# Quarter products in all groups, weights' sums moved into the first layer

## The chip, the cores and the metric

One core of one Trainium2 chip. The metric is the device time of one execution in microseconds (us).

## The reference

Attention in chunks of 32 positions with some context and 8 memory positions, over 4 x 768 tokens and 8 heads of 64; then two layers on its 3072 x 512 result:

```
x = attention(q, k, v, mem_k, mem_v)      # 3072 x 512
h = maximum(x @ w_in, 0)
x = (h * h) @ w_out                       # 512 -> 2048 -> 512
h = x @ w_in2
g = maximum(h, 0) + log1p(exp(-abs(h)))
out = g @ w_out2                          # 512 -> 2048 -> 512
```

All is float32. The kernel splits each operand into a high and a low part that TensorE multiplies fast (F32R) and makes three products for each (low x high, high x high, high x low).

## The kernel before

Tokens go in six blocks of 512 (NB); the second layer joins two blocks to a group (NGR = 3). TensorE (PE) works through block 0 and 1 of the first layer in steps f = 0..15, one tile of 128 hidden columns each, then blocks 2 to 5 in slots (n, p), p = 0..7, two tiles each, then the second layer, which has a first and a second product for each group.

Quarter products: a product of 2 x 2 quarters needs eight quarter products; with sums of quarters of activations and of weights made beforehand, seven do (`order` lists the seven, `quarter` in the first layer and `product` in the second make one). In the kernel before the slots, the first products of all groups and the second products of groups 1 and 2 (`second_stage`) go that way; group 0's second product (`plain_stage`, L1177) makes all eight. In `plain_stage` the sums of the output weights for the later groups are made as well (`add`, `weight_sums`) and stored to DRAM (`wsum`); its 16 weights' tiles come in 8 loads of 1 MB (`wo`), while `second_stage` uses 14 loads of 1 MB. Loads of weights go through four places in turn (`fetch`); x of the next group is loaded and split inside the second product (`next_x`).

The weights of the second layer arrive as 64-bit numbers and are turned into 32-bit ones by three operations (`rebias` on ScalarE, two in `r_join` on VectorE). For the input weights `in_jobs` (L594) does this during the slots of blocks 2 to 4, with the four sums (`four`) and four splits, each with a cast on ScalarE, a subtraction on VectorE and stores. For the output weights `out_jobs` (L648) does it during block 5's eight slots, without sums. `sum_jobs` (L574) makes the sums of the first layer's own weights during block 1's steps; in each slot `sum_load` fetches four of them (`wx`) into one fixed place each. The work buffers of all these are cf0, cf1 and cf2.

All DMAs are issued by SyncE (SP), in one order. VectorE (DVE), ScalarE (ACT) and SP each run their instructions in order too. From block 1's steps on, the instructions are recorded first (class `Recorder`) and then played in an order that is written out by hand as a list of numbers (MOVES, three parts: up to the middle of slot (4, 7), from there to the second layer, and the second layer's first two pairs). Recorded instructions carry L154, the line that plays them, in the profile; the line numbers of `g_split` and its like are those of helpers (`halves` L551, `low_half` L546).

Of the kernel before, what the change touches and what calls it, by code (L numbers as in the profile page):

```python
# [14 lines left out]
ALU = mybir.AluOpType  # L15
# [32 lines left out]
AHEAD = 1  # L48
SOFT_A = ((), (0,), (1, 2), (3, 4), (5, 6), (7, 8), (9, 10), (11, 12))
# [62 lines left out]
""",  # L112
    """
# [10 lines left out]
""",  # L124
    """
42 12 11 12 4 0 14 0 2 3 6 1 1 2 0 0 -38 -31 -24
# [4 lines left out]
class Recorder:  # L131
# [10 lines left out]
    def play(self, moves):  # L142
        jobs, self.jobs = self.jobs, None
        moves = iter(moves.split())
        at, order = 0, []
        for i, (engine, job) in enumerate(jobs):
            if engine is self.nc.tensor:
                order.append((at + 0.5, i))
                at += 1
            else:  # L150
                order.append((at + int(next(moves, 0)), i))
        for _, i in sorted(order):
            engine, job = jobs[i]
            ins = job().ins  # L154
            tile_ = (job.keywords["out"] if "out" in job.keywords else job.args[0]).tensor
            if hasattr(tile_, "tag"):
                name, by, first = self.last.get(tile_.tag, (None, None, None))
                if name != tile_.name:
                    if first is not None and by is not engine:
                        why = mybir.DependencyInfo(mybir.DependencyClass.Sync, mybir.DependencyReason.DATA)  # L160
                        self.tc.add_manual_dep(ins, first.name, why, reason="turn")
                    self.last[tile_.tag] = tile_.name, engine, ins
# [11 lines left out]
def body(ctx: ExitStack, tc: tile.TileContext, qk, vW, w1, w2, out):  # L174
# [347 lines left out]
    wsum = [dram.tile([P, KP, 2, QW], F32R, name=f"wsum{i}") for i in range(4)]  # L522
# [9 lines left out]

    def r_abs(f, top, low):
        rebias(f, top)
# [26 lines left out]
    def split(k, x, *stores):  # L561
        t = cf_tile(k, (P, 2, 2, QW), F32R)
        halves(t[:, :, 0], t[:, :, 1], x, *[(o, t[:, i]) for o, i in stores], late=True)
# [10 lines left out]
    def sum_jobs(p):  # L574
# [13 lines left out]
        def casts():  # L588
            split(kc, d["s"][:, 0:2], (wx[p][:, 0:2], slice(0, 2)))
            split(ka, d["s"][:, 2:4], (wx[p][:, 2:4], slice(0, 2)))  # L590
# [3 lines left out]
    def in_jobs(p):  # L594
        d = {}

        def load(i):
            d["r", i] = r_load(i, 2 * p + i, 0)

        def start(i):  # L600
            if i == 0:
# [769 lines left out]
```

## Time and profile before

| | us |
|---|---|
| median of 3 runs | 1068.08 |
| lowest, highest | 1067.32, 1069.87 |
| the profiled execution | 1067.74 |
| its span, first to last instruction | 1066.0 |

The profile is one execution. Its span is what the views below divide; 1.74 us of the execution's time lie outside it. PE is TensorE's products, PEld its weight loads, which overlap them. The granted clock is 0.998 over the span.

### The profile page before, as it was taken

The numbers are of one execution on the slowest core, as the hardware profiler recorded it, in microseconds if no ns is written. First come the engines' busy times: TensorE is split into PE (matmuls) and PEld (weight loads), VectorE is DVE, ScalarE is ACT, GpSimd is POOL, SyncE is SP. The second block draws the span as 40 slices with busy tenths as digits, with TensorE's granted clock in tenths as the row PEclk, the third lists the DMA queues.
The fourth block names the chain that finished last, engine by engine and source line by source line (L and its number), as shares of the span: only waits on it lengthen the run. The fifth ranks groups of instructions, "written<-read, shape, count | busy, mean of one in ns | idle before, by whom it ended". The sixth has DMA issues, their size and how long they took to land.

```text
span 1066.0 us, 20067 instructions
## 1 busy us (share of the span) xinstructions
PE 1046.4 (98%) x8072; PEld 886.2 (83%) x8072; DVE 767.0 (72%) x1321; ACT 589.7 (55%) x989; POOL 0.7 (0%) x6
## 2 busy tenths in 40 slices
PE   5999999999999999999999999999999999999998
PEld 5788888888888888888898788888788888888886
DVE  6877488788877778866584566967377886477953
ACT  3776554475576567547785654433355545354442
POOL 0000000000000000000000000000000000000000
PEclk9999999999999999999999999999999999999999
DMA  9764253478778678847999645865755757565762
GB/s 359 273 247 163 66 190 136 157 237 295 232 236 292 214 238 254 277 139 226 324 307 345 210 148 177 272 220 166 265 203 200 279 198 257 192 203 180 248 207 99
DMA packets 95196, 238.03 MB, mean 223 GB/s; under 512 B 8064, under 2 KB 40832, under 8 KB 87936
## 3 DMA queue, kind: packets, MB, share of 16 engines
q1 hardware_dynamic: 95104, 236.75, 65.6%
q8 instruction: 64, 1.05, 0.4%
q14 instruction: 28, 0.23, 0.1%
HBM read 184.29 MB, written 52.43 MB: 222 GB/s over the span
## 4 chain that ended last, share of the span: by engine, by line
PE 93%; DVE 3%; DMA 2%; issue 1%; ACT 1%; SPq 0%; ACTq 0%; DVEq 0%
PE acc L154 21%; PE bk L1173 19%; PE bk L1093 19%; PE hq L154 15%; PE hp L154 4%; PE acc L476 4%; PE xs L154 3%; PE bk L154 2%; PE hp L430 2%; PE hp L431 1%; PE hp L432 1%; DVE gl L546 1%; DMA wsum<-cf 1%; PE sc L271 1%; DVE h L1110 1%
## 5 line engine op out<-in xcount | busy, mean ns | idle before, releaser
L154 PE MATMUL acc<-g,w 128*128 128x512 f32 x984 | 257.4, 394 | 0.7 <-ACT g L154 0.3
L1173 PE MATMUL bk<-gh,ws 128*128 128x512 f32 x704 | 217.1, 390 | 0.1
L1093 PE MATMUL bk<-xo,ws 128*128 128x512 f32 x930 | 212.0, 389 | 1.0 <-DMA ws<-wb 1.0
L1093 PEld LDWEIGHTS bk<-xo,ws 128*128 128x128 f32 x930 | 174.5, 188 | 37.6 <-DVE h L1101 1.4
L154 PEld LDWEIGHTS acc<-g,w 128*128 128x128 f32 x984 | 173.9, 189 | 31.0 <-DVE g L154 1.6
L1173 PEld LDWEIGHTS bk<-gh,ws 128*128 128x128 f32 x704 | 131.9, 188 | 28.6 <-ACT cf L1280 0.9
L154 PEld LDWEIGHTS hq<-xe,w 128*128 128x128 f32 x1056 | 140.4, 190 | 11.4 <-ACT r L154 1.9
L154 PE MATMUL hq<-xe,w 128*128 128x256 f32 x1056 | 145.2, 283 | 0.5 <-ACT r L154 0.5
L1173 PE MATMUL bk<-gl,ws 128*128 128x512 f32 x352 | 137.1, 389 | 0.2 <-DVE gl L546 0.2
L546 DVE TENSOR_TENSOR gl<-h,gh 128x1024 fp32r<-128x1024 f32 x72 | 87.8, 1222 | 39.4 <-ACT gh L551 39.1
L551 ACT CAST gh<-h 128x1024 fp32r<-128x1024 f32 x72 | 75.9, 1054 | 68.3 <-PE bk L1173 67.3
L154 ACT ACTIVATE r<-r 128x512 f32<-128x512 f32 x144 | 91.1, 633 | 18.1 <-DVE r L154 15.8
L154 DVE TENSOR_TENSOR g<-r,g 128x512 fp32r<-128x512 f32 x80 | 54.9, 687 | 36.7 <-ACT g L154 36.2
L154 DVE STREAM_TRANSPOSE pt<-t 32x128 f32<-32x128 f32 x256 | 77.5, 303 | 4.2
L154 ACT COPY r<-hq 128x256 f32<-128x256 f32 x128 | 47.2, 369 | 56.8 <-PE hq L154 52.3
L1173 PEld LDWEIGHTS bk<-gl,ws 128*128 128x128 f32 x352 | 66.1, 188 | 14.5 <-DVE gl L546 0.8
L154 DVE TENSOR_TENSOR cf<-cf 128x256 f32<-128x256 f32 (+2 forms) x128 | 65.1, 537 | 8.4 <-ACT cf L154 7.7
L1100 ACT ACTIVATE cf<-cf 128x1024 f32<-128x1024 f32 x47 | 49.9, 1063 | 33.2 <-DVE cf L1099 33.2
L1099 DVE TENSOR_SCALAR cf<-h 128x1024 uint32<-128x1024 uint32 x47 | 32.6, 693 | 42.8 <-ACT h L1114 41.7
L1101 DVE SCALAR_TENSOR_TENSOR h<-h,cf 128x1024 f32<-128x1024 f32 x47 | 57.2, 1218 | 3.4 <-ACT cf L1100 3.4
L154 ACT CAST cf<-cf 128x512 fp32r<-128x512 f32 x64 | 37.5, 592 | 28.4 <-DVE cf L154 19.1
L154 DVE TENSOR_TENSOR r<-hq,r 128x256 f32<-128x256 f32 x96 | 40.3, 421 | 14.5 <-ACT r L154 8.8
(129 smaller groups left out, 1249.5 us busy)
## 6 DMA issues: line engine op xcount, KB each, us to landing
w<-wx SPq DMA_DIRECT2D x128, 256.0 KB, 4.4
ws<-wa SPq DMA_DIRECT2D x24, 1024.0 KB, 7.0
ws<-wo SPq DMA_DIRECT2D x20, 1024.0 KB, 5.9
ws<-wb SPq DMA_DIRECT2D x24, 768.0 KB, 4.3
r<-w SPq DMA_DIRECT2D x16, 1024.0 KB, 6.8
cf<-w SPq DMA_DIRECT2D x32, 512.0 KB, 6.3
ws<-wsum SPq DMA_DIRECT2D x16, 1024.0 KB, 5.2
qk<-qk SPq DMA_DIRECT2D x44, 336.0 KB, 5.3
```

The source lines that it names most:

```text
L154: ins = job().ins
L271: nc.tensor.matmul(out=sv[(2 * c + r) * 32:(2 * c + r + 1) * 32, j, w, i, :], lhsT=t[d, 2 * i + r, c * CHUNK:(c + 1) * CHUNK], rhs=t[d, 2 ...
L430: nc.tensor.matmul(out=hp, lhsT=b, rhs=xh[:, c], start=(c == 0), stop=False)
L431: nc.tensor.matmul(out=hp, lhsT=a, rhs=xl[:, c], start=False, stop=False)
L476: nc.tensor.matmul(out=acc[m][:, cols], lhsT=a, rhs=b, start=(f == 0 and j == 0 and cols.start == 0), stop=(f == KF - 1 and j == 2),)
L546: nc.vector.tensor_tensor(out=lo, in0=x, in1=hi.bitcast(F32), op=ALU.subtract)
L551: nc.scalar.copy(out=hi, in_=x)
L1093: nc.tensor.matmul(out=bk, lhsT=a, rhs=b, start=(start and n == 0), stop=(n == 5), skip_group_check=not start)
L1099: nc.vector.tensor_scalar(z.bitcast(U32), h.bitcast(U32), 1 << 31, None, op0=ALU.bitwise_or)
L1100: nc.scalar.activation(out=z, in_=z, func=AF.Softplus)
L1101: nc.vector.scalar_tensor_tensor(out=h, in0=h, scalar=0.0, in1=z, op0=ALU.max, op1=ALU.add)
L1173: nc.tensor.matmul(out=bk, lhsT=a, rhs=b, start=(start and j == 0), stop=(stop and j == 2), skip_group_check=more)
```

## The change

Group 0's second product uses `second_stage` like the others, and `plain_stage` is gone, with its sums of weights. All of the output weights' preparation is in the first layer now: `in_jobs` and `out_jobs` are replaced by `word_jobs`, sixteen rounds of one pair of tiles each (8 for the input weights, 8 for the output weights with their sums), recorded at the slots that WORDS lists. Rounds take turns between two sets of buffers, cf0 to cf2 and cf3 to cf5. POOL's scratch area for DMAs is cut to 1024. All three parts of MOVES are new, and `play` reads them differently: before, a number counted PE's instructions from the place of recording; now it counts places in the list of all recorded instructions, and PE's instructions fill what is left, in their order of recording. `wsum` is one tensor, and the second sum and the third have changed places in it.

```
+WORDS = [2 * r for r in range(11)] + [24, 25, 27, 28, 30]
...
 MOVES = (
...
+492 504 522 522 526 531 575 595 537 528 548 610 615 623 630 700 716 722 712 718 723 728 6 12 8 15 24 -16 -10 3 9 14 25
...
+28 35 41 39 45 21 22 -22 0 12 22 -1125 -1130 -1024 -1040 -922 -1032 -1049 -939 -902 -755 -751 -888 -904 -874 -859 -870
+-764 -761 -747 -731 -726 -725 -707 -697 -629 2 5 11 17 -65 -39 -24 -14 22 4 11 9 16 24 8 17 22 -101 -82 -69 -58 27 16
...
+26 38 36 18 28 -1250 -1257 -1159 -1154 -1147 -1176 -1160 -1155 -1137 -1119 -1117 -1125 -1150 -1146 -1142 -1094 -1017
+-1013 -1071 -1016 -1010 -945 -937 -878 -884 1 21 23 30 39 2 9 11 12 44 20 29 24 30 35 28 31 37 -19 -8 15 28 -21 -9 15
...
     def play(self, moves):
         jobs, self.jobs = self.jobs, None
         moves = iter(moves.split())
-        at, order = 0, []
-        for i, (engine, job) in enumerate(jobs):
-            if engine is self.nc.tensor:
-                order.append((at + 0.5, i))
-                at += 1
-            else:
-                order.append((at + int(next(moves, 0)), i))
-        for _, i in sorted(order):
+        order = [None] * len(jobs)
+        for i, (engine, _) in enumerate(jobs):
+            if engine is not self.nc.tensor:
+                order[i + int(next(moves, 0))] = i
+        rest = (i for i, (engine, _) in enumerate(jobs) if engine is self.nc.tensor)
+        for i in order:
+            i = next(rest) if i is None else i
...
+    def word_jobs(r):
+        layer_in, r = r < KP, r % KP
+        part = 0 if layer_in else 1
+        q, j = divmod(r, 2)
+        tiles = (2 * r, 2 * r + 1) if layer_in else (4 * q + j, 4 * q + 2 + j)
+        ka, kb, kc = ((0, 1, 2), (3, 4, 5))[r % 2]
+        f = None
+        raws = [r_load(k, t, part) for k, t in zip((ka, kb), tiles)]
+        f = cf_tile(kc)
+        for i in range(2):
+            rebias(f[:, i], raws[i][0])
+            r_join(f[:, i], *raws[i])
+        f = f.rearrange("p i (h q) -> p i h q", h=2)
+        s = cf_tile(ka, (P, 4, QW))
+        if layer_in:
             four(s, f)
...
+            split(kb, f[:, :, 1], (wb[r][:, 0:2], slice(0, 2)))
             t = f[:, 1].bitcast(F32R)
...
+            halves(t[:, 0], t[:, 1], f[:, 0, 0], (wa[r][:, 0], t))
+            split(kb, s[:, 0:2], (wa[r][:, 1:3], slice(0, 2)))
+            split(kc, s[:, 2:4], (wa[r][:, 3:4], slice(0, 1)), (wb[r][:, 2:3], slice(1, 2)))
+        else:
+            four(s, f.rearrange("p i h q -> p h i q"))
+            split(kb, f[:, :, 0], (wo[:, 0, 2 * q:2 * q + 2, j], slice(0, 2)))
+            t = f[:, 0].bitcast(F32R)
+            halves(t[:, 0], t[:, 1], f[:, 1, 1], (wo[:, 1, 2 * q + 1, j], t))
+            split(kb, s[:, 0:2], (wsum[:, 0:2, r], slice(0, 2)))
+            split(kc, s[:, 2:4], (wsum[:, 2:4, r], slice(0, 2)))
...
             old = life.pop() if life else None
-            jobs = (jobs2 if n < NB - 1 else jobs3) if here else []
+            if here:
+                at_slot = (n - 2) * KP + p
+                for r in [r for r in range(2 * KP) if WORDS[r] == at_slot]:
+                    word_jobs(r)
...
-        sums = {4: 0, 5: 1, 6: 2, 2: 3}
+        sums = {4: 0, 5: 1, 6: 3, 2: 2}
...
-                if grp > 0 and f % 4 == 3:
+                if f % 4 == 3:
...
-                (second_stage if grp else plain_stage)(grp, first_stage(grp))
+                second_stage(grp, first_stage(grp))
...
-    nc = bacc.Bacc("TRN2", target_bir_lowering=False, num_devices=1)
+    nc = bacc.Bacc("TRN2", target_bir_lowering=False, num_devices=1, dynamic_dma_scratch_size=1024)
```

A round records 25 instructions that are not PE's. The rows of numbers shown end with round 0's, and hold round 1's (-1125 to -629) and round 3's (-1250 to -884).

## Rows read from the trace of the kernel before

**Rows 1.** Page of the profile: busy us, share of the span, instructions of each engine.

```profile
PE 1046.4 (98%) x8072; PEld 886.2 (83%) x8072; DVE 767.0 (72%) x1321; ACT 589.7 (55%) x989; POOL 0.7 (0%) x6
```

**Rows 2.** Busy time by stage: length, then PE, PEld, DVE, ACT, POOL (instructions), clock, DMA.

```profile
0.00:124.00 124.00, 110.71 (x1440) 91.95 (x1441) 89.11 (x146) 77.94 (x130) 0.70 (x6) 0.99 0.64 233
124.00:220.00 96.00, 96.00 (x902) 78.98 (x901) 75.94 (x173) 47.69 (x87) 0.00 (x0) 1.00 0.47 162
220.00:316.00 96.00, 95.75 (x1119) 85.16 (x1117) 77.67 (x185) 61.02 (x124) 0.00 (x0) 1.00 0.76 249
...
508.00:604.00 96.00, 95.12 (x551) 82.59 (x550) 55.15 (x102) 66.85 (x128) 0.00 (x0) 1.00 0.90 301
...
831.00:909.00 78.00, 77.78 (x342) 63.65 (x341) 61.81 (x68) 40.75 (x50) 0.00 (x0) 1.00 0.72 255
```

**Rows 3.** The chain that ended last: start, length, engine and products.

```profile
609.12 57.12 PE bk L1093 x252
...
670.32 73.79 PE bk L1173 x324
```

**Rows 4.** PE in order of time: the slots' first product, and two slots of block 5.

```profile
218.96 0.87 PE L154 MATMUL hq<-xe,w 128*128 128x256 f32 x6
...
487.05 1.60 PE L154 MATMUL hq<-xe,w 128*128 128x256 f32 x12
...
497.61 1.59 PE L154 MATMUL hq<-xe,w 128*128 128x256 f32 x12
```

**Rows 5.** PE in order of time: first products of the three second stages.

```profile
666.07 0.62 PE L1173 MATMUL bk<-gh,ws 128*128 128x512 f32 x2
...
830.88 0.62 PE L1173 MATMUL bk<-gh,ws 128*128 128x512 f32 x2
...
984.05 0.62 PE L1173 MATMUL bk<-gh,ws 128*128 128x512 f32 x2
```

**Rows 6.** All engines in order of time, end of group 0; in brackets idle time and releaser.

```profile
755.32 0.32 SPq L525 DMA_DIRECT2D wsum<-wq  x1
...
761.14 0.60 SPq L525 DMA_DIRECT2D ws<-wb  x1
...
766.86 1.40 PE L1093 MATMUL bk<-xo,ws 128*128 128x512 f32 x5 [1.01 <-DMA ws<-wb]
```

**Rows 7.** DVE's and ACT's groups by form: count, busy us, mean ns of one.

```profile
L154 DVE TENSOR_TENSOR cf<-cf 128x512 fp32r<-128x512 f32 x56 | 38.0, 688 | 8.0 <-ACT cf L154 7.7
L154 DVE TENSOR_TENSOR cf<-cf 128x256 f32<-128x256 f32 x64 | 25.0, 419 | 0.4
L154 DVE SCALAR_TENSOR_TENSOR cf<-cf 128x512 uint32<-128x512 uint32 x32 | 21.8, 688 | 3.1 <-ACT cf L154 2.7
...
L154 DVE TENSOR_SCALAR cf<-cf 128x512 uint32<-128x512 uint32 x32 | 13.6, 424 | 10.1 <-DMA w<-wx 3.9 <-DMA cf<-w 3.6 <-DMA wo<-cf 2.5
...
L154 DVE TENSOR_TENSOR cf<-cf 128x256 fp32r<-128x256 f32 x8 | 3.3, 415 | 0.0
...
L154 ACT CAST cf<-cf 128x512 fp32r<-128x512 f32 x56 | 34.3, 620 | 28.1 <-DVE cf L154 18.7 <-DMA wb<-cf 4.1 <-DVE s L317 2.0
```

**Rows 8.** Busy time by stage, columns as in rows 2: the stretch in block 1.

```profile
157.00:196.00 39.00, 39.00 (x385) 32.11 (x383) 31.46 (x73) 18.67 (x33) 0.00 (x0) 1.00 0.37 129
196.00:212.00 16.00, 16.00 (x174) 13.12 (x159) 13.44 (x35) 6.52 (x14) 0.00 (x0) 1.00 0.49 161
```

**Rows 9.** The same in stretches of 12 us: two of DVE's fullest.

```profile
220.00:232.00 12.00, 11.75 (x134) 10.16 (x133) 11.61 (x28) 7.59 (x16) 0.00 (x0) 1.00 0.60 192
...
316.00:328.00 12.00, 12.00 (x79) 10.72 (x73) 11.63 (x31) 10.03 (x21) 0.00 (x0) 1.00 0.79 263
```

**Rows 10.** Waits of SP's queue: total us, times, longest.

```profile
SPq L154 <- DVE cf L154: 60.3, 38, 9.7
```

**Rows 11.** DMA issues: count, KB each, median us to landing.

```profile
w<-wx SPq DMA_DIRECT2D x128, 256.0 KB, 4.4
```

**Rows 12.** Instructions on wsum: duration ns (min, median, max), first and last start us.

```profile
L525 SPq DMA_DIRECT2D ws<-wsum x16: 320/332/887, 837.9 to 1043.2; - x16
```

More of the change, by code (lines that the diff above doesn't have):

```diff
@@ L75 @@
     """
[36 rows of a table removed]
-""",
-    """
[10 rows of a table removed]
[41 rows of a table added]
+""",
+    """
[12 rows of a table added]
 """,
     """
-42 12 11 12 4 0 14 0 2 3 6 1 1 2 0 0 -38 -31 -24
+6 1 2 2 2 2 -26 2 4 4 4 4 4 4 4 3 -52 -48 -43
 """,
@@ L521, in body @@
     wo = dram.tile([P, 2, KP, 2, 2, QW], F32R, name="wo")
-    wsum = [dram.tile([P, KP, 2, QW], F32R, name=f"wsum{i}") for i in range(4)]
+    wsum = dram.tile([P, 4, KP, 2, QW], F32R, name="wsum")
     def store(out, in_):
@@ L531, in r_load @@
         return v[:, :, 1], v[:, :, 0]
-    def r_abs(f, top, low):
-        rebias(f, top)
     def r_join(f, top, low):
@@ L559, in flush, with split @@
             lows.pop(0)()
-    def split(k, x, *stores):
+    def split(k, x, *stores, late=False):
         t = cf_tile(k, (P, 2, 2, QW), F32R)
-        halves(t[:, :, 0], t[:, :, 1], x, *[(o, t[:, i]) for o, i in stores], late=True)
+        halves(t[:, :, 0], t[:, :, 1], x, *[(o, t[:, i]) for o, i in stores], late=late)
     def four(s, f):
@@ L588, in casts @@
         def casts():
-            split(kc, d["s"][:, 0:2], (wx[p][:, 0:2], slice(0, 2)))
-            split(ka, d["s"][:, 2:4], (wx[p][:, 2:4], slice(0, 2)))
+            split(kc, d["s"][:, 0:2], (wx[p][:, 0:2], slice(0, 2)), late=True)
+            split(ka, d["s"][:, 2:4], (wx[p][:, 2:4], slice(0, 2)), late=True)
         return [((), (), (words,), ()), ((), (), (sums,), (casts,))]
[L594 to L601, printed above, removed]
-                d["f"] = cf_tile(2)
-            r_abs(d["f"][:, i], *d["r", i])
-        def join(i):
-            r_join(d["f"][:, i], *d["r", i])
-        def sums():
-            f = d["f"].rearrange("p i (h q) -> p i h q", h=2)
-            s = d["s"] = cf_tile(0, (P, 4, QW))
+    def word_jobs(r):
[13 more added lines that the diff above has]
+        if layer_in:
@@ L611, in sums @@
             four(s, f)
-        def casts():
-            f = d["f"].rearrange("p i (h q) -> p i h q", h=2)
-            split(1, f[:, :, 1], (wb[p][:, 0:2], slice(0, 2)))
+            split(kb, f[:, :, 1], (wb[r][:, 0:2], slice(0, 2)))
             t = f[:, 1].bitcast(F32R)
-            halves(t[:, 0], t[:, 1], f[:, 0, 0], (wa[p][:, 0], t), late=True)
-        def last():
-            split(1, d["s"][:, 0:2], (wa[p][:, 1:3], slice(0, 2)))
-            split(2, d["s"][:, 2:4], (wa[p][:, 3:4], slice(0, 1)), (wb[p][:, 2:3], slice(1, 2)))
@@ L623, in call @@
-        def call(fn, *a):
-            return (lambda: fn(*a),)
-        return [
-            (call(load, 0), (), (), ()),
-            (call(load, 1), call(start, 0), call(join, 0), ()),
-            ((), call(start, 1), call(join, 1), ()),
-            ((), (), (sums,), (casts,)),
-            ((), (), (), (last,)),
-        ]
-    out_raw = {}
-    def out_place(f, shape, dtype):
-        if f % 3 < 2:
-            return cf_tile(f % 3, shape, dtype)
-        return late[0].tile(list(shape), dtype, tag="cf", name="cf")
@@ L641, in out_load @@
-    def out_load(f):
-        if f < KF:
-            t = out_place(f, (P, DM), I64)
-            nc.sync.dma_start(out=t, in_=w2[f][:, DM:])
-            v = t.bitcast(U32).rearrange("p (n t) -> p n t", t=2)
-            out_raw[f] = v[:, :, 1], v[:, :, 0]
-    def out_jobs(f):
-        d = {}
-        def start():
-            d["x"] = cf_tile(2, (P, DM))
-            r_abs(d["x"], *out_raw[f])
-        def join():
-            r_join(d["x"], *out_raw.pop(f))
-        def cast():
-            t = out_place(f, (P, 2, 2, QW), F32R)
-            halves(t[:, :, 0], t[:, :, 1], d["x"].rearrange("p (m q) -> p m q", m=2), (wo[:, :, f // 2, f % 2], t), late=True)
-        return (lambda: out_load(f + 1),), (start,), (join,), (cast,)
+            halves(t[:, 0], t[:, 1], f[:, 0, 0], (wa[r][:, 0], t))
@@ L664, in body @@
     jobs1 = [j for p in range(KP) for j in sum_jobs(p)]
-    jobs2 = [j for p in range(KP) for j in in_jobs(p)]
-    jobs3 = [out_jobs(f) for f in range(KF)]
     xo = {}
@@ L867, in octet @@
             return [(lambda w=w: add(w)) if isinstance(w, str) else (lambda w=w: part(w)) for w in what]
-        none = ((), (), (), ())
         visits = {(0, "end"): (None, 0), (2, "mid"): (0, 1), (3, "end"): (1, 2), (5, "mid"): (2, 3), (6, "end"): (3, None)}
@@ L942, in slot @@
             old = life.pop() if life else None
-            jobs = (jobs2 if n < NB - 1 else jobs3) if here else []
+            if here:
+                at_slot = (n - 2) * KP + p
+                for r in [r for r in range(2 * KP) if WORDS[r] == at_slot]:
+                    word_jobs(r)
             todo = [(f, (m,)) for f in pending[:1 if (n, p) == (2, 0) else 2] for m in range(4)]
             del pending[:1 if (n, p) == (2, 0) else 2]
-            e1 = take(jobs)
-            e2 = none if here and n < NB - 1 and p in (3, 6) else take(jobs)
-            if (n, p) == (NB - 2, KP - 1):
-                assert not jobs2
-                e2 = ((lambda: out_load(0),), (), (), ())
             outs(2)
@@ L962, in slot @@
             flush()
-            run(e1[0])
             at_point(1)
@@ L968, in slot @@
             at_point("a1")
-            run(e1[1])
             if old:
@@ L1000, in slot @@
             at_point(2)
-            run(e1[2])
             if old:
@@ L1007, in slot @@
                 nc.vector.tensor_tensor(out=or1[:, half[1]], in0=oa, in1=or1[:, half[1]], op=ALU.add)
-            run(e1[3])
             outs(1)
@@ L1013, in slot @@
             flush()
-            run(e2[0])
             at_point(3)
@@ L1026, in slot @@
                 nc.vector.tensor_tensor(out=r0[:, half[0]], in0=a, in1=r0[:, half[0]], op=ALU.add)
-            run(e2[1])
             at_point(4)
-            run(e2[2])
-            run(e2[3])
             if here and n == NB - 1:
@@ L1053, in body @@
                 loads += [((grp, "a", p), wa[p]), ((grp, "b", p), wb[p])]
-            if grp == 0:
-                loads += [((grp, "o", p), wo[:, :, p]) for p in range(KP)]
-            else:
-                for i in order:
-                    for h in range(2):
-                        if i in sums:
-                            src = wsum[sums[i]][:, 4 * h:4 * h + 4]
-                        else:
-                            m, k = ((0, 0), (0, 1), None, (1, 1))[i]
-                            src = wo[:, m, 4 * h + k:4 * h + 4:2]
-                        loads.append(((grp, i, h), src))
+            for i in order:
+                for h in range(2):
+                    if i in sums:
+                        src = wsum[:, sums[i], 4 * h:4 * h + 4]
+                    else:
+                        m, k = ((0, 0), (0, 1), None, (1, 1))[i]
+                        src = wo[:, m, 4 * h + k:4 * h + 4:2]
+                    loads.append(((grp, i, h), src))
         early_places = [([wpool], "w8"), ([wpool], "w10"), ([xpool], "xl"), ([wpool], "w12")]
@@ L1175, in three @@
                 )
-        def plain_stage(grp, prev):
-            banks = {}
-            todo = next_x(grp + 1, ((1, 3, 8), (8, 9, 14)))
-            words = {}
-            def add(p):
-                w = ws[grp, "o", p]
-                t = words[p % 2] = cf_tile(p % 2, (P, 2, 2, QW))
-                nc.vector.tensor_tensor(
-                    out=t, in0=w[:, :, :, 0].bitcast(F32), in1=w[:, :, :, 1].bitcast(F32), op=ALU.add
-                )
-            def weight_sums(q):
-                (a11, a21), (a12, a22) = ((words[k][:, 0], words[k][:, 1]) for k in range(2))
-                nc.vector.tensor_tensor(out=a22, in0=a21, in1=a22, op=ALU.add)
-                minus(a21, a11, a21)
-                minus(a11, a22, a11)
-                minus(a12, a12, a11)
-                for i, x in enumerate((a22, a11, a21, a12)):
-                    t = late[0].tile([P, 2, 2, QW], F32R, tag="ev", name="wq") if i % 2 else cf_tile(2, (P, 2, 2, QW), F32R)
-                    halves(t[:, :, 0], t[:, :, 1], x, (wsum[i][:, 2 * q:2 * q + 2], t))
-            g_split((grp, 0), ht[0][:, 0])
-            soft_steps(grp, 13, 14)
-            for f in range(KF):
-                p, i = divmod(f, 2)
-                w = ws[grp, "o", p]
-                if f + 1 < KF:
-                    g_split((grp, f + 1), ht[(f + 1) // 2][:, (f + 1) % 2])
-                if i == 0:
-                    add(p)
-                if f % 4 == 2:
-                    weight_sums(f // 4)
-                for job in todo.get(f, ()):
-                    job()
-                gh, gl = gs.pop((grp, f))
-                for t in range(2):
-                    for m in range(2):
-                        for s in range(2):
-                            if f == 0:
-                                banks[t, m, s] = bank()
-                            three(
-                                banks[t, m, s], [w[:, m, i, j, s * P:(s + 1) * P] for j in range(2)],
-                                gh[:, t], gl[:, t], f == 0, f == KF - 1,
-                            )
-                            if f == KF - 1:
-                                if s:
-                                    e = tmp("ev")
-                                    nc.vector.tensor_copy(e, banks[t, m, s])
-                                else:
-                                    e = cf_tile((2 * t + m) % NCF)[:, 0]
-                                    nc.scalar.copy(out=e, in_=banks[t, m, s])
-                                store_out(m, s, grp, t, e)
-                    if f == 0 and t == 0:
-                        last_product(grp, *prev)
-                        soft_steps(grp, 15)
-                if i:
-                    fetch()
@@ L1315, in body @@
             slot(NB - 1, KP + 1, False)
-            assert not jobs2 and not jobs3
             flush()
```

94 rows, old and new, of the table MOVES are left out of this document.

## The prediction

> **What bounds the kernel now.** I read the busy times first: PE is busy 1046.4 of 1066.0 us [rows 1]. A busy PE need not be a PE at its pace, so I took the pace next, from the chain that ended last: 252 products of 512 columns in 57.12 us are 226.7 ns each, and 324 in the group's second product 227.7 ns [rows 3]. Two slots of the first layer start 10.56 us apart [rows 4], and a slot holds 24 products of 512 columns and 42 of 256: 24 x 0.2267 = 5.44 leaves 5.12 us for 42, 122 ns each, just over half the price of a product of twice the columns. So PE runs at one pace almost everywhere, and what is left is idle time. The table by stage finds it: 13.29 us in the first 124 us, nothing from 124 to 220, 0.25 in the next stretch, 0.88 from 508 to 604, and 0.22 in group 1's second product [rows 2]; another 1.01 us stands at 766.86 [rows 6], and the rest is the tail after the last product. The bound is the number of products that PE makes. DVE is the engine next to it: 75.94 of 96 us in the stretch from 124, 77.67 in the one behind [rows 2], and in its fullest 12 us 11.61 and 11.63 [rows 9].
>
> **The change, part by part.**
>
> *Group 0's second product.* The old form makes 16 x 2 x 2 x 2 x 3 = 384 products of 512 columns, the quarter form 7 x 4 x 2 x 2 x 3 = 336. That is 48 fewer, at 226.7 ns [rows 3] 10.88 us. The trace also has the direct comparison, since groups 1 and 2 already go this way: from the start of one group's second product to the start of the next one's it is 830.88 - 666.07 = 164.81 us for group 0 and 984.05 - 830.88 = 153.17 us for group 1 [rows 5]. The difference, 11.64 us, holds the 10.88, plus a stall of 1.01, less 0.22 that group 1 waits for DVE [rows 2, 6]. After the change group 0 runs group 1's code, the next group's inputs among it, with the same number of loads behind it, so I take 11.64.
>
> *Why the 1.01 us goes.* At the end of the old stage the last sums of weights are stored at 755.32 and all results are stored at once; SP issues the load of the next weights only at 761.14, behind them, and PE waits for it at 766.86 [rows 6]. The quarter form stores its results in several places of the stage. At the end of group 1, PE does not wait for that load. If the stall stayed, the sum would be 1.0 us less.
>
> *A price that could be doubted.* The row gives 226.7 ns for one product in a dense stream [rows 3], and this stands in the sum. The Trainium skill ("TensorE: Matmul & The Clock Gate", Back-to-back issue gap) gives two other figures for 512 columns: some 216 ns by its formula, and 131 ns sustained in a real kernel. By these the 48 products would be worth 10.4 or 6.3 us (estimates from that page); the trace disagrees with the second by far, in a stream of pairs of weight load and product, and the trace decides.
>
> *What the quarter form adds beside PE.* More splits of activations, sums of activations, and 14 loads where there were 8; what goes is the summing and splitting of weights. Group 1 shows the new mixture: DVE 61.81 of 78 us, ACT 40.75, PE idle 0.22 [rows 2]. I cost it at nothing beyond that 0.22, which the 11.64 already has.
>
> *Weights' sums in the first layer.* PE's own order there is unchanged: the recorder takes its instructions in the order of recording. So nothing is gained but the idle 0.25 and 0.88 [rows 2], at most 1.13 us. What is added lies on DVE, ACT and SP. One pair of output tiles costs DVE, old: 2 x (424 + 688) for the joins and 2 x 688 for the splits, 3.60 us. New: the same joins, 4 x 419 for the sums, and splits of 3 x 688 + 415, 6.38 us [rows 7]. Eight pairs: 8 x 2.78 = 22.2 us more DVE. ACT gets 512 + 256 columns a pair more, under 2 x 620 ns [rows 7], 9.9 us at most in all. A pair of input tiles is 6.38 us before and after. Averaged over 124 to 604 this is easy: 22.2 us in 480. But it is not spread evenly, so the places count.
>
> *Where the rounds go.* The moves in the diff give this. Behind 124 us the three engines retire 2590 instructions in 192 us [rows 2], 13.5 per us, and with SP's issues I take 14. Slot 0 begins just ahead of the product at 218.96, and a slot lasts 10.6 us without attention [rows 4] and nearer 12 with it; slot 2 is then near 240 and slot 6 near 287. Round 1, recorded at slot 2, is moved by -1125 to -629 places: some 160 to 195 us. Round 3, at slot 6, by -1250 to -884: 198 to 224 us. So the odd rounds, on the new buffer set, start in block 1's steps, where before no such work was, and the eleven rounds of this part have about 26 us each. In block 5 five rounds stand where eight pairs stood: 5 x 6.38 = 31.9 against 8 x 3.60 = 28.8 us, under a DVE that has 55.15 of 96 [rows 2], with fewer loads and stores than before.
>
> *The tight place* is 157 to 212 us. DVE has 31.46 + 13.44 = 44.90 us there [rows 8]; round 1 adds 6.38 and the part of round 3 before 212 some 2.8: 54.1 of 55 us. The fullest rows ran at 11.6 of 12, which for 55 us is 53.3, so 0.8 us is over. At such a load PE lost 0.25 us in one row and nothing in the other [rows 9]. Some sums for the slots' weights move later in the new order, which gives room; the new order also changes every other wait, which can cost. The cost of the whole re-ordering lies between -1.13 (all idle time gone) and +4.6 (half of the 9.2 us falls where PE waits for DVE). I take +0.6, near the excess and near the full rows.
>
> *Smaller edits.* The weights' sums in one tensor instead of four change addresses, not sizes. The smaller scratch area for POOL's DMAs pays for the second buffer set; every DMA in this kernel is issued by SP, so it costs nothing. The copies of the low halves are now recorded at once instead of late, but the moves place them anyway.
>
> **Sum.** 1066.0 - 11.64 + 0.6 = 1055.0 us of span. The profiled execution took 1067.74, 1.74 outside its span, and the median of the three runs is 1068.08, 0.34 above it. So 1055.0 + 1.74 + 0.34 = 1057.0 us, with +0 to +2.5 us of new stalls as the forecast's own spread (1056.4 to 1059).
>
> **Rivals.** First, *DVE becomes the bound in block 1's steps.* For it: the 98% worked out above over 55 us, where no stretch of the old trace was so full for so long. Against it: PE ran on beside 97% in 12 us [rows 9], and PE looks two tiles ahead there. With 4.6 us in place of 0.6 the time is 1061.0; the case reaches from 1059 to 1064.
>
> Second, slower: *SP's one queue.* A round's stores wait for DVE's low halves, and behind them stand the reloads of the summed weights, one place for each, needed once a slot. A place is free after 6 products of 256 columns (0.7 us) and its load lands after 4.4 us [rows 11]; in a slot of 10.56 [rows 4] about 5.4 us of slack is left. The longest wait of SP for DVE's cf was 9.7 us [rows 10]. Where such a wait stands ahead of a reload, PE stands still for 9.7 - 5.4 = 4.3 us. The point is the fourth such round: 4 x 4.3 = 17.2, 1074 us, slower than before. Against it: the old trace has 38 waits of that kind, and PE's idle time behind 124 us shows no wait for such a reload. Two or three such rounds (8.6 to 12.9 us) give 1065 to 1069, no change that counts.
>
> Third, *the change doesn't do what it says*: group 0 waits for sums that are not there. In group 1 the first load of a sum is issued at 837.9 [rows 12], 7 us into the stage, so in group 0 near 673. The last round is recorded in slot 30, near 575 us, and moved by at most some 220 places, ending near 600. With 70 us to spare I give it no chance of its own.
>
> Fourth, *more than counted*: all of the 1.13 us goes (1066.0 - 11.64 - 1.13 + 2.08 = 1055.3), and waits hidden in PE's pace with it; under 1054.8.
>
> **How the numbers follow.** Chances: forecast 0.66, DVE bound 0.17, no net change 0.04, SP's queue 0.06, more than counted 0.07. About 0.3% of 1068 is 3.2 us, what a measurement here can tell from no change. Faster by over that: 0.66 + 0.17 + 0.07 = 0.90; within it 0.04; slower 0.06. The range goes from 1054.8, half a us under the time with all idle time gone, to 1063, most of the first rival: it leaves out the two last kinds on the upper side, 0.10, a few hundredths of the first rival, and the fourth.
>
> **What would show it.** From group 0's second product to group 1's 153 us instead of 164.81; 336 products and 6 more, no store of sums behind 660 us, no wait for ws<-wb. Between 124 and 604 PE idle of about 1 to 2 us; DVE near 97% from 157 to 212. The start of group 0's second product stays near 666 or up to 2 us later. Wrong would be a start behind 668 (rival one or two: the releaser named at PE's gaps tells them apart, DVE g or r against DMA w<-wx), or a group 0 stage longer than group 1's.

## The result, and the profile after

| | before | after |
|---|---|---|
| median, us | 1068.43 (1067.32 to 1069.87) | 1058.19 (1055.01 to 1058.98) |
| the profiled execution, us | 1067.74 | 1058.98 |
| its span, us | 1066.0 | 1057.2 |

The ratio is 0.9898, with a 95% interval of 0.9874 to 0.9922: 10.2 us less (8.3 to 13.5 by the interval), where 11.1 were forecast (1057.0). Medians do not settle a part of an us; what follows goes by stages of the profiles. The page of the profile after gives each engine's busy time, its share of the span and its instructions:

```profile
PE 1035.4 (98%) x8024; PEld 877.0 (83%) x8024; DVE 791.1 (75%) x1359; ACT 604.8 (57%) x1005; POOL 0.7 (0%) x6
```

PE has exactly 48 products fewer than in [rows 1] and 11.0 us less busy time; DVE has 24.1 us more, ACT 15.1. PE in order of time: the first product of block 1's steps, then the first of each group's second product:

```profile
126.60 2.88 PE L161 MATMUL acc<-g,w 128*128 128x512 f32 x12
...
669.03 0.62 PE L1120 MATMUL bk<-gh,ws 128*128 128x512 f32 x2
...
822.22 0.62 PE L1120 MATMUL bk<-gh,ws 128*128 128x512 f32 x2
...
975.42 0.61 PE L1120 MATMUL bk<-gh,ws 128*128 128x512 f32 x2
```

The same block 1 product in the kernel before:

```profile
124.02 2.88 PE L154 MATMUL acc<-g,w 128*128 128x512 f32 x12
```

These few rows split the difference between the two profiles. From group 0's second product to group 1's it is now 822.22 - 669.03 = 153.19 us where [rows 5] have 164.81: 11.62 less. From block 1's steps to group 0's second product it is 669.03 - 126.60 = 542.43 where it was 666.07 - 124.02 = 542.05: 0.38 more. And block 1's steps began 2.58 us later. 11.62 - 0.38 - 2.58 = 8.66, of the 8.8 us between the two spans.

Busy time by stage, with the columns of rows 2: first the stretches that answer to rows 2, then those that answer to rows 8.

```profile
124.00:220.00 96.00, 96.00 (x900) 78.87 (x899) 83.74 (x189) 54.52 (x98) 0.00 (x0) 1.00 0.60 203
220.00:316.00 96.00, 94.32 (x1045) 83.18 (x1044) 83.14 (x196) 63.47 (x129) 0.00 (x0) 1.00 0.86 291
...
508.00:604.00 96.00, 95.90 (x567) 84.56 (x566) 60.69 (x117) 68.00 (x132) 0.00 (x0) 1.00 0.83 286
...
157.00:196.00 39.00, 39.00 (x293) 32.19 (x292) 36.43 (x86) 21.26 (x37) 0.00 (x0) 1.00 0.54 195
196.00:212.00 16.00, 16.00 (x191) 13.17 (x190) 15.25 (x38) 8.22 (x16) 0.00 (x0) 1.00 0.71 226
```

PE idles 1.68 us in the stretch from 220, where it idled 0.25, and 0.10 from 508, where it idled 0.88. Another 0.24 us stands at 377. The 1.68 are two waits for DVE (PE in order of time, the wait in brackets):

```profile
267.51 0.98 PE L161 MATMUL hq<-w,w 128*128 128x256 f32 x6 [0.43 <-DVE r L161]
...
291.95 0.50 PE L161 MATMUL acc<-g,w 128*128 128x512 f32 x1 [1.25 <-DVE g L161]
```

### The profile page after: what moved, and what is told of

It is laid out like the page before. It is cut to its first block, busy times and chain, and to the rows that moved or that the text cites. A ratio compares the mean times of both kernels' runs of the same rounds, so it can differ in the third digit from the quotient of the medians.

```text
span 1057.2 us, 19995 instructions
## 1 busy us (share of the span) xinstructions
PE 1035.4 (98%) x8024; PEld 877.0 (83%) x8024; DVE 791.1 (75%) x1359; ACT 604.8 (57%) x1005; POOL 0.7 (0%) x6
## 4 chain that ended last, share of the span: by engine, by line
PE 87%; DVE 8%; issue 2%; ACT 2%; DMA 1%; SPq 0%; DVEq 0%; ACTq 0%
PE bk L1040 20%; PE acc L161 19%; PE bk L1120 18%; PE hq L161 13%; PE hp L161 4%; PE acc L483 3%; PE xs L161 2%; PE bk L161 2%; DVE gl L550 2%; PE hp L437 1%; PE hp L438 1%; PE hp L439 1%; DVE h L1057 1%; DVE pt L161 1%; DVE cf L161 1%
## 5 line engine op out<-in xcount | busy, mean ns | idle before, releaser
L1120 PE MATMUL bk<-gh,ws 128*128 128x512 f32 x672 | 207.3, 390 | 0.1
L1120 PEld LDWEIGHTS bk<-gh,ws 128*128 128x128 f32 x672 | 125.9, 188 | 27.3 <-ACT cf L1168 1.4
L555 ACT CAST gh<-h 128x1024 fp32r<-128x1024 f32 x84 | 88.6, 1055 | 85.0 <-PE bk L1120 84.8
L550 DVE TENSOR_TENSOR gl<-h,gh 128x1024 fp32r<-128x1024 f32 x84 | 102.5, 1222 | 42.3 <-ACT gh L555 41.9
L1120 PE MATMUL bk<-gl,ws 128*128 128x512 f32 x336 | 131.1, 390 | 0.3 <-DVE gl L550 0.3
L161 DVE TENSOR_TENSOR cf<-cf 128x256 f32<-128x256 f32 (+2 forms) x176 | 84.9, 517 | 2.1 <-ACT cf L161 0.8
L1120 PEld LDWEIGHTS bk<-gl,ws 128*128 128x128 f32 x336 | 63.1, 188 | 14.6 <-DVE gl L550 1.5
L161 ACT CAST cf<-cf 128x512 fp32r<-128x512 f32 (+1 forms) x80 | 45.1, 577 | 23.4 <-DVE cf L161 21.0
L161 ACT CAST g<-r 128x512 fp32r<-128x512 f32 x80 | 49.8, 622 | 2.5
```

What stands on the lines that cost most here:

```text
L550: nc.vector.tensor_tensor(out=lo, in0=x, in1=hi.bitcast(F32), op=ALU.subtract)
L555: nc.scalar.copy(out=hi, in_=x)
L1120: nc.tensor.matmul(out=bk, lhsT=a, rhs=b, start=(start and j == 0), stop=(stop and j == 2), skip_group_check=more)
```

## The experiments

Three things were open: whether the second product carries all of the gain, and why PE's 1.01 us went; whether DVE is at its limit in the steps and slots, or single places of the order cost the little that was lost; and whether the 2.58 us at the start belong to the change.

### The new first layer with the old second product

> The new first layer with the old form of group 0's second product (384 products in place of 336), without its sums of weights, which the first layer has made; its weights are loaded in the same sizes from the upper half of the output weights alone, so group 0's results are others. From the start of group 0's second product to group 1's: theory A (the 1.01 us stall came from the eight stores of results that were issued together at the stage's end) 153.2 + 10.9 + 1.0 = 165 us, PE waiting about 1 us for ws<-wb; rival B (it came from the sums' stores, which waited for DVE) 164.0 us and no such wait. Against the changed kernel 10.9 to 11.9 us more: 1069 to 1070 us.

```diff
-                second_stage(grp, first_stage(grp))
+                (second_stage if grp else plain_stage)(grp, first_stage(grp))
...
+                loads += [((grp, "o", p), wo[:, 0, p // 2 * 2:p // 2 * 2 + 2]) for p in range(KP)]
```

Measured: 1065.58 us (1063.81 to 1071.85). PE, first products of group 0's and group 1's second products, and between them SP in order of time at group 0's end:

```profile
666.60 0.62 PE L1122 MATMUL bk<-gh,ws 128*128 128x512 f32 x2
...
830.12 0.62 PE L1122 MATMUL bk<-gh,ws 128*128 128x512 f32 x2
```

```profile
751.37 0.34 SPq L1117 DMA_DIRECT2D out<-cf  x1
...
756.23 0.33 SPq L1117 DMA_DIRECT2D out<-ev  x1
756.66 0.40 SPq L532 DMA_DIRECT2D ws<-wb  x1
```

SP in the kernel before, the first and the last of the eight results:

```profile
755.69 0.42 SPq L1168 DMA_DIRECT2D out<-cf  x1
...
760.45 0.60 SPq L1168 DMA_DIRECT2D out<-ev  x1
```

The stage takes 163.52 us: the two forms, 48 products apart, differ by 163.52 - 153.19 = 10.33 us, and the other 1.29 of the 11.62 went with the sums. The eight results are still stored together, but the load behind them is issued at 756.66, where it was 761.14 in [rows 6], and PE waits for nothing there. The times of rival B came: without the work on sums the bunch of results makes no wait. Before, the first result was stored only behind the last sum (755.32), and the eight results then filled SP up to the load. So the sums are needed for the wait; that the bunch has no part in it is not shown, since no run has the sums without the bunch. Nor does this run separate the sums' stores on SP from their work on DVE and ACT.

In time it took 7.4 us more than the changed kernel in the same series (1058.20), where 10.9 to 11.9 were expected. The stage was 0.6 us less than the expected 10.9 more, and most of the rest is the start: block 1's steps began at 123.41 in this profile and at 126.45 in the other.

### The old first layer with the new second product

> The old first layer and old order with the quarter form in all groups; the sums of output weights are made nowhere, and plain weights of the same size are loaded in their place, so the results are others. It is the second product's part alone. If it carries all of the gain (theory), 1068.4 - 11.6 = 1056.8 us, from group 0's second product to group 1's 153.2 us, PE idle between 124 and 604 us 1.1 us as before. If the first layer's new order brought part of the gain, it stays above 1058.2; if that order costs several us, it falls below 1055.

```diff
-            if grp == 0:
-                loads += [((grp, "o", p), wo[:, :, p]) for p in range(KP)]
...
+                    m, k = ((0, 0), (0, 1), (1, 0), (1, 1))[i % 4]
+                    loads.append(((grp, i, h), wo[:, m, 4 * h + k:4 * h + 4:2]))
```

Measured: 1056.56 us, ratio 0.9898 (0.9875 to 0.9921), as good as the whole change's. PE's rows:

```profile
667.79 0.62 PE L1166 MATMUL bk<-gh,ws 128*128 128x512 f32 x2
...
822.20 0.62 PE L1166 MATMUL bk<-gh,ws 128*128 128x512 f32 x2
```

So the second product carries the gain by itself, and the new first layer, which makes the sums that this run leaves out, brings nothing that can be seen. The stage was not the expected 153.2 us but 822.20 - 667.79 = 154.41. PE waits twice for a low half in its first third, 0.17 and 0.52 us; the rest of the 1.2 us is not explained:

```profile
697.95 0.50 PE L1166 MATMUL bk<-gl,ws 128*128 128x512 f32 x1 [0.52 <-DVE gl L546]
```

### More DVE work where DVE is fullest

> The changed kernel with the additions and subtractions on DVE of rounds 1 and 3 made twice, with the same results: 2 x (4 x 419 + 3 x 688 + 415) ns = 8.3 us more DVE between 157 and 226 us, where DVE was busy 51.7 of 55 us (157 to 212). Theory (DVE stands just short of its limit there, with work for later behind it that can slide): PE idles 0 to 2 us more, time within 2 us of the changed kernel. Rival (already at the limit, every us more is PE's): 5 to 8 us more.

```diff
             ins = job().ins
+            if i in twice:
+                job()
...
                     word_jobs(r)
+                    if r in (1, 3):
+                        nc.twice |= {...}
```

Measured: 1065.06 us, 6.9 more than the changed kernel in the same series (1058.20). By stage it is 676.12 - 126.72 = 549.4 us, 7.0 more:

```profile
126.72 2.88 PE L162 MATMUL acc<-g,w 128*128 128x512 f32 x12
...
676.12 0.62 PE L1127 MATMUL bk<-gh,ws 128*128 128x512 f32 x2
```

The rival's size came, not the theory's: of 8.3 us added, 7.0 came back as time. Busy time in two stretches of 10 us, this run, and then the changed kernel:

```profile
210.00:220.00 10.00, 8.38 (x84) 6.48 (x83) 9.47 (x28) 3.44 (x7) 0.00 (x0) 0.78 0.42 159
220.00:230.00 10.00, 9.28 (x39) 7.35 (x38) 9.75 (x16) 7.87 (x16) 0.00 (x0) 0.88 0.92 306
```

```profile
210.00:220.00 10.00, 10.00 (x104) 8.13 (x104) 9.10 (x18) 7.28 (x15) 0.00 (x0) 1.00 0.59 175
220.00:230.00 10.00, 10.00 (x122) 8.81 (x121) 9.40 (x20) 6.94 (x14) 0.00 (x0) 1.00 0.83 283
```

PE loses 1.62 + 0.72 us to waits there, five of them for the transposes ahead of the attention's small products. And the granted clock (the number behind POOL's) falls to a mean of 0.78 and 0.88, with a stretch at 0.50, 1.2 GHz, behind the five waits. PE from 124 to 604 us, this run and the changed kernel, then this run's page and the stretch at half clock:

```profile
124.00:604.00 480.00, 475.73 (x4596) 415.70 (x4595) 386.29 (x872) 305.15 (x597) 0.00 (x0) 0.99 0.73 247
124.00:604.00 480.00, 477.98 (x4625) 417.93 (x4624) 380.15 (x858) 310.07 (x605) 0.00 (x0) 1.00 0.74 248
```

```profile
PE 1040.0 (98%) x8024; PEld 879.8 (83%) x8024; DVE 799.1 (75%) x1375; ACT 604.3 (57%) x1005; POOL 0.7 (0%) x6
...
217.00:220.00 3.00, 3.00 (x30) 2.45 (x27) 2.97 (x8) 1.93 (x4) 0.00 (x0) 0.50 0.00 0
```

PE idles 4.27 us where it idled 2.02, so 2.25 us more, close to the 0 to 2 of the theory; the larger part, 4.6 us, is busy time, with as many products (1040.0 against 1035.4). So the time is not "every us more is PE's", us for us: short waits came with products that took longer, in part at half clock.

### The same added work where DVE looked free

> The changed kernel with DVE's additions and subtractions of rounds 11 to 15 made twice, same results: 5 x 4.155 = 20.8 us more DVE in block 5, where DVE was busy 60.7 of 96 us. Theory (an added us of DVE costs PE only where DVE is full, as with rounds 1 and 3): less than 1 us more than the changed kernel. Rival (each round's chain has a due time, and DVE's share tells nothing): 5 us more or above.

```diff
-                    if r in (1, 3):
+                    if r in (11, 12, 13, 14, 15):
```

Measured: 1063.71 us, ratio to the kernel before 0.9965 (0.9945 to 0.9986); from block 1's steps to group 0's second product it is 674.44 - 123.01 = 551.4 us, 8 to 9 more than the changed kernel (542.43 and, with an early start, 543.14):

```profile
123.01 2.88 PE L162 MATMUL acc<-g,w 128*128 128x512 f32 x12
...
674.44 0.62 PE L1127 MATMUL bk<-gh,ws 128*128 128x512 f32 x2
```

My theory falls, and the rival's "5 us more or above" came. DVE was busy 60.7 of 96 us over block 5, but not evenly. Stretches of 12 us, this run, then the changed kernel in its last profile (e11_after below), in which block 1's steps start within 1 us of this run's:

```profile
544.00:556.00 12.00, 10.40 (x64) 8.87 (x63) 11.55 (x26) 8.32 (x18) 0.00 (x0) 1.00 0.71 228
556.00:568.00 12.00, 10.85 (x60) 9.70 (x60) 10.48 (x19) 9.46 (x18) 0.00 (x0) 0.86 0.76 256
...
580.00:592.00 12.00, 12.00 (x71) 10.46 (x71) 7.82 (x16) 6.41 (x13) 0.00 (x0) 1.00 0.97 315
```

```profile
544.00:556.00 12.00, 12.00 (x77) 10.82 (x76) 10.30 (x20) 11.37 (x24) 0.00 (x0) 1.00 0.93 330
556.00:568.00 12.00, 12.00 (x75) 10.74 (x74) 10.30 (x22) 9.19 (x18) 0.00 (x0) 1.00 0.86 310
```

DVE had 1.7 us to spare in each of these two, and the written order puts the rounds right there. Its free time behind them (4.2 us in the stretch from 580) did not help: PE waits for the g and r of its own tiles, which stand behind the doubled additions in DVE's order (before the 1.60 us wait at 555.70, DVE makes six additions on cf in a row, from 552.32, and then g). That fits the rival's due times; how much of the cost is a full DVE and how much the place in the order is not separated. From 124 to 604 PE idles 7.1 us, where it idles 1.8 in the changed kernel's last profile; the rest of the 8 us is busy time, with the granted clock at 0.86 in the second stretch.

### The sums on POOL

> The changed kernel with the four sums of each of the sixteen rounds made on POOL in place of DVE, same results and same places in the order: DVE has 16 x 1.68 = 26.8 us less. Theory (DVE's fullness in the steps and slots makes the small waits that are left): PE idle from 124 to 604 us falls from 2.0 us to 1 or less, time 0 to 1.5 us less. Rival (POOL's additions are slower, hold up DVE or a round's chain): several us more.

```diff
-            nc.vector.tensor_tensor(out=out, in0=a, in1=b, op=op)
+            (by or nc.vector).tensor_tensor(out=out, in0=a, in1=b, op=op)
...
-            four(s, f)
+            four(s, f, nc.gpsimd)
```

Measured: 1060.08 us (0.9921, 0.9900 to 0.9941), not better; from block 1's steps to group 0's second product 667.91 - 123.43 = 544.5 us, 1 to 2 more. POOL's group (count, busy us, mean ns) and the stretch from 220:

```profile
L161 POOL TENSOR_TENSOR cf<-cf 128x256 f32<-128x256 f32 x64 | 60.5, 962 | 509.6 <-DVE cf L161 447.1 <-DMA w<-wx 52.7 <-ACT r L161 8.3
...
220.00:316.00 96.00, 93.03 (x1041) 82.04 (x1040) 78.21 (x178) 62.42 (x126) 14.97 (x16) 1.00 0.85 283
```

DVE has 4.9 us less in this stretch than after the change, and PE idles more, 2.97 us. A sum takes 962 ns on POOL against 419 on DVE [rows 7], which makes a round's chain longer. And DVE did not get as light as planned: over the whole program it is busy 781.2 us against 791.1, 9.9 us less where 26.8 were taken off it. Others of its additions and subtractions took longer in this run; one group, in the changed kernel and in this run:

```profile
L161 DVE TENSOR_TENSOR cf<-cf 128x512 fp32r<-128x512 f32 x64 | 42.8, 685 | 0.5 <-ACT cf L161 0.3
```

```profile
L161 DVE TENSOR_TENSOR cf<-cf 128x512 fp32r<-128x512 f32 x64 | 49.6, 792 | 5.1 <-ACT cf L161 4.7
```

So this run is no test of a DVE that is lighter by 26.8 us, and whether DVE's fullness makes the small waits stays open.

### The order of recording

> The changed kernel with all three lists of moves empty, so that every instruction is issued in the order of recording: what the written order is worth. Theory (rounds as one lump of 25 instructions hold up DVE, ACT and SP ahead of what PE needs): at least 50 us more than the changed kernel. Rival (the order matters little, since PE's is the same): less than 10 us more.

```diff
-MOVES = (...)
+MOVES = ("", "", "")
```

Measured: 1290.54 us in one execution. PE's longest waits by releaser (total us, times, longest):

```profile
PE hq L100 <- ACT r L100: 193.6, 16, 20.8
PE hq L100 <- DVE r L100: 5.3, 4, 1.9
```

Sixteen waits, as many as rounds: 25 instructions in a lump come with a wait of PE of some 12 us each time. The whole written order is worth 232 us, by this one execution. The 193.6 us of waits are most of it; the rest is PE's busy time, 1072.6 us against 1035.4 with as many products, at a mean granted clock of 0.92.

### One wait taken out of the order, twice

> The changed kernel with one low half (g) on DVE, and its cast on ACT, put five transposes earlier in the written order, the one for which PE waited 1.25 us at 291.95. Theory (that wait is the order's, eight transposes of 2.5 us ahead of g): from block 1's steps to group 0's second product 542.4 - 1.2 = 541.2 us, no such wait, 1057.0 us in the median if the first 124 us are the same. Rival (DVE is full there, and the wait moves to the next low half): 542.4 us, with another wait of about 1 us within 20 us behind it.

```diff
+            at = [1860, 1863, 1866, 1868, 1870, 1873, 1878]
+            put = [order[i] for i in at]
+            put = [put[3], put[6], put[0], put[1], put[2], put[4], put[5]]
```

> The changed kernel with both operations that PE needs there, the low half g and the addition r behind it, put ahead of five of the eight transposes (moving g alone had moved PE's wait to that r, 1.48 us). Theory (the wait is the order's): neither of the two waits, no new one of over 0.5 us up to 316 us, and from block 1's steps to group 0's second product about 1.4 us less than with g alone (542.9): 541.5 us. Rival (DVE's total is what counts there, the wait moves on again): 542.4 us or more, with a wait of 1 us or more by 316 us.

```diff
+            behind = [order[i] for i in (1860, 1863, 1866, 1870, 1873)]
+            order[1860:1884] = [i for i in order[1860:1884] if i is None or i not in behind] + behind
```

Measured: 1055.90 (0.9889, 0.9868 to 0.9909) and 1055.61 (0.9890, 0.9863 to 0.9916); the changed kernel itself had 1055.37 beside the second. PE's rows around 290 us, first of the one, then of the other:

```profile
289.64 0.98 PE L167 MATMUL hq<-w,w 128*128 128x256 f32 x6 [1.48 <-DVE r L167]
```

```profile
291.24 0.98 PE L164 MATMUL hq<-w,w 128*128 128x256 f32 x6 [1.04 <-DVE r L164]
```

The wait for g is gone in both and another one of 1 to 1.5 us stands in its place, in both; the stretch from block 1's steps to group 0's second product is 666.72 - 123.85 = 542.9 and 665.74 - 121.62 = 544.1 us (the second with a wait of 0.87 for a load of weights in group 0's first product). The rivals' outcomes came: these two changes of a few places moved the wait and did not remove it. That DVE's total is the reason is not shown by them. Neither can be told from the changed kernel in its time.

### The changed kernel again, for its start

> The changed kernel again, unedited, for the spread of the first 124 us. Theory (the 2.6 us by which block 1's steps started late in the first profile came from a longer stretch at half clock ahead of 50 us, not from the change): a profile with a shorter stretch at half clock starts block 1 near 124 us and has a span near 1054.5. Rival (the change delays the start): block 1 starts near 126.6 us at any clock.

> The changed kernel unedited, beside the other of this call. The stretch from block 1's steps to group 0's second product 542.4 us; block 1 starts near 123.5 us where the first 124 us are at full clock and near 126.5 us where two stretches of them are at half clock; median about 1058.

Measured: 1058.20 us (0.9908, 0.9890 to 0.9926) and 1055.37 us (0.9885, 0.9858 to 0.9912). The first series' profile has the long stretch at half clock again, with block 1's steps at 126.45 and a span of 1057.0. The second has none. Its rows of PE, among them a wait in group 0's first product, and then the stretch from 30 to 60 us in the kernel before, in the changed kernel's first profile, and in this one:

```profile
122.18 2.88 PE L161 MATMUL acc<-g,w 128*128 128x512 f32 x12
...
658.38 7.10 PE L1040 MATMUL bk<-xo,ws 128*128 128x512 f32 x30 [0.73 <-DMA ws<-wb]
...
665.32 0.61 PE L1120 MATMUL bk<-gh,ws 128*128 128x512 f32 x2
...
819.05 0.61 PE L1120 MATMUL bk<-gh,ws 128*128 128x512 f32 x2
```

```profile
30.00:60.00 30.00, 28.49 (x269) 24.07 (x257) 26.05 (x44) 24.36 (x41) 0.00 (x0) 0.94 0.72 261
```

```profile
30.00:60.00 30.00, 27.17 (x246) 23.08 (x247) 23.42 (x38) 22.27 (x38) 0.00 (x0) 0.89 0.65 226
```

```profile
30.00:60.00 30.00, 29.04 (x264) 24.25 (x265) 26.18 (x44) 24.11 (x40) 0.00 (x0) 1.00 0.73 263
```

The same program starts block 1's steps at 126.60, 126.45 or 122.18 us, with a granted clock of 0.89 in that stretch in the first profile and 1.00 in the last. The kernel before, at 0.94, lies between. With the old first layer the late start comes too (125.93 in that run's profile). So the 2.58 us are not the change's. Group 0's stage is 153.21 us in the first of these profiles and 819.05 - 665.32 = 153.73 in the second, which has a wait of 0.29 for a load of ws<-wb behind it, at 774.09.

## Why the prediction was right

The forecast was 1057.0 with a range of 1054.8 to 1063; measured were medians of 1058.19, 1058.20 and 1055.37. The last lies below the forecast's own spread (1056.4 to 1059): how long the start ran at half clock differs from execution to execution, and the forecast had no term for it. That the first two came so near 1057.0 is luck in that part.

**The products.** 11.64 us by stage were forecast, 11.62 measured. That the two agree to 0.02 us is luck: the changed kernel's three profiles give 11.62, 11.60 and 11.08, and the old first layer with the same second product 10.40. But the stage of group 1 in the old trace did tell what group 0's would be, waits among it. The split that the prediction gave, 10.88 for the products and 1.01 for the stall less 0.22, was less exact: the run with the old second product measured 10.33 for the two forms, 48 products apart, and 1.29 for what went with the sums. The Trainium skill's 131 ns for a product ("TensorE: Matmul & The Clock Gate", Back-to-back issue gap) would have given 6.3 us, and its formula 10.4 (estimates from that page). The 10.33 rule out the first and do not tell the second from 10.88.

**The reason for the 1.01 us** was wrong as it stood. I put it on the results, which the old stage stores all at once. With the results still stored at once and only the sums gone, the load came 4.5 us earlier and PE did not wait. The step had the right sum since both go with the old stage; what spreading out the results alone would have brought, with the sums left in, no run shows.

**The first layer.** +0.6 us was forecast, +0.38 measured at a late start of block 1's steps (0.3 in the second profile). At an early one, 665.32 - 122.18 = 543.1 us, it is 1.1, of which 0.73 is the wait for a load of weights in group 0's first product: part of what was won at the start was given back there. The tight place was named rightly in kind and not in position. DVE got 36.43 + 15.25 = 51.7 of 55 us between 157 and 212 where 54.1 were worked out: two of the ten additions on the first layer's weights (cf<-w) have left it, and the joins of one round alone stand in it. PE lost nothing there; it lost 1.68 us 55 to 80 us later, at 267 and 291, for which the prediction had only the remark that the new order changes every other wait.

**How near the first rival was** came out only by the doses. I held half of an excess possible (4.6 us); 8.3 us more DVE in two rounds cost 7.0, and 20.8 us in five rounds cost 8 to 9; in both, waits were a part and products that took longer the rest. The change had almost no margin left, in places where the share over 96 us said it had a third. The rival with SP's queue did not appear: the only waits of PE for a reload of summed weights (w<-wx) in the profiles with the written order are two of 0.3 us, one in each of the runs with places of the order changed.

**What stays open.** The two waits of 1.68 us in the slots: sums on POOL made them longer, with DVE's other additions slower beside it, and two changes of the order moved the larger one. Whether another order removes them was not found. Why the start of the program gets half clock for longer in some executions is open as well; the runs show only that it does not depend on this change.

## What to carry to other kernels

Where a later stage already runs the form that a change gives to an earlier one, take the time of that stage, from start to start, rather than counting instructions: it holds the waits too. Judge whether an engine has room by stretches as short as the work that waits for it (12 us here), not over a stage, and by what stands ahead of that work in its order. Where the order of issue is written by hand, the order is the resource: 22 us of added work cost 0.3 to 1.1 us with it, and leaving out the whole of it, the old work's order too, cost 232.

## What was not expected of the hardware

Idle time of PE cost more than itself: after waits of 0.2 to 0.4 us between products of 32 columns around 215 us the granted clock fell to half, a mean of 0.78 over 10 us. The same fall shows at 0.86 in block 5 behind waits of 0.4 to 1.6 us, between products of 256 and 512 columns. A sum of 256 columns took 962 ns on POOL, 2.3 times DVE's 419 (spans on POOL are rough). And in that run DVE's subtractions on cf took 792 ns on average instead of 685, while its additions r<-hq,r, with one input from TensorE's results, stayed at 418 (421 before); the mechanism is not shown.
